# Attention and feed-forward on one core: the first pairs pinned in program order, values on four array tiles, second weights in three areas

## The chip, the core and the metric

The kernel runs on one core of a Trainium2 chip. The metric is the device time of one execution in microseconds. The core has five engines that the text names: TensorE (PE; its weight loads are PEld), VectorE (DVE), ScalarE (ACT), GpSimd (POOL) and SyncE (SP), whose queue issues all the DMAs here.

## The reference, cut to what matters

```python
scores = scale * np.matmul(q, k.transpose(0, 1, 3, 2))      # 8 batches, 8 heads, 576 positions, 64 wide
rel = pos[:, None] - pos[None, :]
mask_local = (rel >= 0) & (rel < 32)                        # heads 0 to 3
mask_strided = (rel >= 0) & (pos[None, :] % 32 == pos[:, None] % 32)   # heads 4 to 7
attn = softmax(np.where(masks, scores, -1e9))
x = (attn @ v).transpose(0, 2, 1, 3).reshape(4608, 512)
h = x @ w_in                                                # 512 x 2048
g = h * (1.0 / (1.0 + np.exp(-1.702 * h)))
return g @ w_out                                            # 2048 x 512
```

## The kernel before, in words

**Attention** is cut into 48 pairs of two units each (`_pairs`, line 55): for each of the eight batches three strided pairs and three local ones, in turn. A unit is a third of the positions of a batch (local) or a sixth of the residues (strided), of four heads. For a pair `scores` (169) multiplies queries and keys in windows into two PSUM banks; `softmax` (185) is a generator in five parts: mask and maximum on VectorE, subtraction on GpSimd (L212), exp on ScalarE (L214), sum and reciprocal on VectorE (L216 to L218), multiplication on GpSimd (L220). `turn` (223) transposes the probabilities on TensorE and copies them (L230). `values` (232) multiplies them with the values into one bank, and ScalarE copies the result into the five areas of x (L258, L267). The two heads of a group, j = 0 and 1, lie on partitions 0 to 63 and 64 to 127 of queries, keys, probabilities and values, and the result of head j goes to partitions 64j to 64j+63: a 64x64 tile of the array on its diagonal.

**The first product** (x with w_in) is done with seven products in place of eight, each in three terms of high and low halves (`product`, 330; 42 matmuls of 288 columns a block). There are eight blocks of w_in (pairs of 128 columns) and eight batches: 64 block products, numbered n, in passes of eight. `combine` (344) adds the seven up and writes the hidden rows to DRAM. `x_part` (282) splits the seven inputs of a batch, `x_sums` (277) makes two of the sums in them.

**Weights** come as 64-bit words, one block a megabyte: `w_convert` (300) makes them 32-bit floats, two operations on ScalarE (L303, L304) and one on VectorE (L307); `w_sums` (311) makes four sums on GpSimd (L316); `w_split` (320) splits all seven into high and low, two casts on ScalarE (L325) and two subtractions (L327), one of 768 columns on GpSimd and one of 1024 on VectorE. Raw blocks and split blocks share a pool of nine slots. The w_out blocks are read into the arena, over areas that attention no longer needs (`raw_at`, 105).

**The second product** (18 sets of 256 rows, four steps each) reads the hidden rows back (`load_g`, 467), applies the activation, sums and splits them (`prep`, 480) and multiplies with w_out (`products`, 508; `finish`, 522).

**The order.** The six pairs of batch 0 come first, in a loop of their own (line 394), with weight blocks 0 and 1 among them. The rest is a list of steps (line 551): a step holds one of the seven products of a block, and `side` (425) hangs other work on a step: the pairs of the next batch, the preparation of w_in blocks 2 to 7 in pass 0, that of the w_out blocks in the last pass. Only matmuls and transposes are kept in the order written (`keep_in_program_order` ties an instruction to the one written just ahead of it on its engine). All else is put into each engine's order by the framework's planner, which goes by its own estimate of times, takes work that is ready, and prefers what was written earlier.

Of the kernel before, what the change touches and what calls it, by code (L numbers as in the profile page):

```python
# [9 lines left out]
F32 = mybir.dt.float32  # L10
# [58 lines left out]
def attn_ffn(ctx, tc, qk, vs, weights, masks, ident, out):  # L69
# [6 lines left out]
    vector, scalar, gpsimd, sync = nc.vector, nc.scalar, nc.gpsimd, nc.sync  # L76

    def matmul(*args, **kw):
        tc.keep_in_program_order(nc.tensor.matmul(*args, **kw))  # L79

    def transposed(*args, **kw):
        tc.keep_in_program_order(nc.tensor.transpose(*args, **kw))
# [12 lines left out]
    prs = cut(AT_PR, 512, 2)  # L95
# [50 lines left out]
    qks, vts = {}, {}  # L146

    def load_qk(p):
        if p < len(pairs):
            nq, nk = _size(pairs[p][0])  # L150
            n = 4 * (nq + nk)
            t = qks_at[p % 2][:, :n]
            qks[p] = t.rearrange("p (i n) -> p i n", i=4)
            sync.dma_start(out=t, in_=qk[p][:, :n])

    def load_v(p):
        if p < len(pairs):
            n = 4 * (3 if pairs[p][0] == "l" else 2) * D
            t = vts_at[p % 2][:, :n]
# [25 lines left out]
    def softmax(p, banks):  # L185
        kind, _, c = pairs[p]
        nq, nk = (QL, WL) if kind == "l" else (QS, WS)
        pr = prs[p % 2].rearrange("p (i j n) -> p i j n", i=4, j=2)
        heads = prs[p % 2].rearrange("p (h n) -> p h n", h=8)[:nq, :, :nk]
# [33 lines left out]
    def turn(p, bank):  # L223
        nq = _size(pairs[p][0])[0]
        for i in range(4):
            transposed(
                bank[:, i * nq : (i + 1) * nq], prs[p % 2][:nq, i * P : (i + 1) * P],
# [4 lines left out]
    def values(p, bank):  # L232
# [5 lines left out]
        for i in range(4):  # L238
            for w, (q0, n, _, nk) in enumerate(windows(kind)):
                o = i * n0 + (q0 if kind == "l" else w * WS)  # L240
                if kind == "s":
                    n = min(n0, (w + 1) * WS) - w * WS
                for j in range(2):
                    rows = slice(j * D, j * D + nk)
                    matmul(
                        bank[j * D : (j + 1) * D, o : o + n],
                        lhsT=v[rows, i, w, :], rhs=pt[rows, i * nq + q0 : i * nq + q0 + n],
                        start=True, stop=True,
                    )
        x = {k: xr[k].rearrange("p (g n) -> p g n", g=2) for k in ("11", "12", "21", "22")}  # L250
        if kind == "l":
            src = bank[:, : 4 * QL].rearrange("p (g u n) -> p g u n", g=2, u=U)
            for h, cs in (("11", [c + u for u in range(U) if c + u < 3]),
                          ("21", [c + u for u in range(U) if c + u >= 3])):
                if cs:
                    u0, o = cs[0] - c, cs[0] % 3 * QL
                    n = len(cs)
                    scalar.copy(  # L258
                        out=x[h][:, :, o : o + n * QL].rearrange("p g (u n) -> p g u n", u=n),
                        in_=src[:, :, u0 : u0 + n],  # L260
                    )
            return
        n, r0, half = U * RES[c], R0[c], NPOS // 2
        src = bank[:, : 4 * n0].rearrange("p (g r t) -> p g t r", g=2, r=n)
        for k, h in enumerate(("12", "22")):
            o = x[h].rearrange("p g (t r) -> p g t r", r=STRIDE)[:, :, :, r0 : r0 + n]
            scalar.copy(out=o, in_=src[:, :, k * half : (k + 1) * half])  # L267
# [102 lines left out]


    load_qk(0)
# [11 lines left out]

    load_w(0)
    load_w(1)
    all_banks = [m_banks[i][x] for x in ("mx", "my", "mz") for i in range(2)]

    def start_banks(p):
        return all_banks[2 * (p % 2) : 2 * (p % 2) + 2]  # L390
# [277 lines left out]
```

## Time and profile before

| | us |
|---|---|
| median of three runs | 964.99 |
| lowest and highest run | 962.55, 965.57 |
| the profiled execution | 962.21 |
| its span on the core | 960.4 |
| TensorE busy in the span | 869.0 |
| VectorE, ScalarE, GpSimd busy | 619.5, 431.3, 501.9 |

The profile is of one execution. The span is what the engines' records cover; about 2 us of the execution's time lie around it. Busy time is the union of an engine's instructions; a matmul's end is modelled, so a busy TensorE is not one at its peak. The passes can be told apart by the writes of hidden rows: the windows below are cut where the writes of blocks 7 and 47 had been issued, at the first product (84.00), at the last pass and at the second stage.

### The profile page before, as it was taken

To read this page: it belongs to the slowest core of one execution; us is meant where nothing else is said; L and a number is where in the kernel's file an instruction comes from. 1 tells how busy PE (TensorE), PEld (TensorE's weight loads), DVE (VectorE), ACT (ScalarE), POOL (GpSimd) and SP (SyncE) were. 2 spreads that over 40 slices of the span, in tenths; PEclk is the share of its full clock that TensorE was granted. 3 is DMA by queue.
4 is the path that set the end of the run, shared out by engine and by line. 5 is a ranking of instruction groups with operands and counts; after the bars stand their busy time and mean duration, and the time that the engine had idled before them with its cause. 6 is when DMAs were issued, how large, how long until landed. Compare 5 with 4: busy or idle time off the path is not lost. (4 is left out here: it accounts for less than half of the span.)

```text
span 960.4 us, 23493 instructions
## 1 busy us (share of the span) xinstructions
PE 869.0 (90%) x9744; PEld 841.1 (88%) x9744; DVE 619.5 (64%) x1055; ACT 431.3 (45%) x733; POOL 501.9 (52%) x486
## 2 busy tenths in 40 slices
PE   3027999999999999999998985999999999999998
PEld 2026999999999999999998985999999999999998
DVE  5776548566474575754755786576767767677665
ACT  4644324233242232322424565555656556564552
POOL 5984213222132132222322699787777877877763
PEclk9999999999999999999999998899999999999999
DMA  9232444544444444354444575344343443434431
GB/s 374 94 112 65 158 148 159 165 162 147 153 159 146 157 162 153 131 178 146 160 137 141 205 252 170 100 145 141 117 136 123 146 142 113 140 121 145 142 110 44
DMA packets 78282, 141.68 MB, mean 148 GB/s; under 512 B 5856, under 2 KB 42848, under 8 KB 76128
## 3 DMA queue, kind: packets, MB, share of 16 engines
q1 hardware_dynamic: 78176, 140.19, 43.8%
q8 instruction: 76, 1.25, 0.5%
q14 instruction: 30, 0.25, 0.1%
HBM read 92.98 MB, written 47.19 MB: 146 GB/s over the span
## 5 line engine op out<-in xcount | busy, mean ns | idle before, releaser
L79 PE MATMUL my<-xa,w 128*128 128x288 f32 x1152 | 186.5, 303 | 10.3 <-ACT xa L272 4.4
L499 DVE TENSOR_TENSOR xa<-arena,xa 128x512 fp32r<-128x512 f32 (+1 forms) x144 | 140.8, 1005 | 81.7 <-ACT xa L498 81.3
L79 PEld LDWEIGHTS my<-xa,w 128*128 128x128 f32 x1152 | 162.6, 191 | 14.4 <-ACT xa L272 4.8
L484 ACT ACTIVATE arena<-arena 128x1024 f32<-128x1024 f32 x72 | 76.4, 1061 | 142.9 <-DMA arena<-hid 136.9
L79 PE MATMUL mx<-xa,w 128*128 128x288 f32 x768 | 129.4, 304 | 2.2 <-ACT arena L354 1.9
L79 PE MATMUL mz<-xa,w 128*128 128x288 f32 x768 | 126.9, 301 | 1.1 <-DVE arena L351 1.1
L212 POOL TENSOR_TENSOR arena<-arena,nmax 128x432 f32<-128x432 f32 (+1 forms) x48 | 51.4, 1070 | 140.4 <-DVE nmax L206 138.5
L351 DVE TENSOR_TENSOR arena<-my,arena 128x288 f32<-128x288 f32 x192 | 85.4, 452 | 49.1 <-PE my L79 48.7
L79 PEld LDWEIGHTS mx<-xa,w 128*128 128x128 f32 x768 | 110.0, 192 | 5.3 <-ACT arena L354 2.6
L79 PEld LDWEIGHTS mz<-xa,w 128*128 128x128 f32 x768 | 109.0, 190 | 2.8 <-DVE arena L351 1.7
L351 DVE TENSOR_TENSOR arena<-mz,arena 128x288 f32<-128x288 f32 x128 | 57.9, 453 | 80.1 <-PE mz L79 79.0
L220 POOL TENSOR_TENSOR arena<-arena,rinv 128x432 f32<-128x432 f32 (+1 forms) x48 | 50.7, 1055 | 110.9 <-DVE rinv L218 92.0
L491 POOL TENSOR_TENSOR arena<-arena 128x256 f32<-128x256 f32 x72 | 60.6, 842 | 84.1 <-DVE xa L499 55.7
L79 PEld LDWEIGHTS s<-arena 64*64 64x64 f32 (+2 forms) x3600 | 90.4, 133 | 15.4 <-issue 13.6
L79 PE MATMUL s<-arena 64*64 64x32 f32 (+4 forms) x3600 | 102.2, 227 | 0.2 <-DMA arena<-vs 0.2
L498 ACT CAST xa<-arena 128x512 fp32r<-128x512 f32 (+1 forms) x144 | 91.0, 685 | 11.2 <-POOL arena L494 10.3
L79 PE MATMUL my<-w,xa 128*128 128x256 f32 x576 | 84.4, 282 | 9.5 <-ACT xa L498 7.2
L499 DVE TENSOR_TENSOR ga<-arena,ga 128x512 fp32r<-128x512 f32 (+2 forms) x72 | 72.3, 1029 | 29.1 <-ACT ga L498 28.9
L79 PEld LDWEIGHTS my<-w,xa 128*128 128x128 f32 x576 | 75.2, 190 | 10.0 <-ACT xa L498 7.4
L79 PE MATMUL mx<-w,xa 128*128 128x256 f32 x576 | 83.8, 281 | 0.0
L79 PE MATMUL mz<-w,xa 128*128 128x256 f32 x576 | 83.7, 281 | 0.0
L492 POOL TENSOR_TENSOR arena<-arena 128x256 f32<-128x256 f32 x72 | 82.7, 1148 | 0.0
(71 smaller groups left out, 1445.8 us busy)
## 6 DMA issues: line engine op xcount, KB each, us to landing
hid<-arena SPq DMA_DIRECT2D x64, 576.0 KB, 3.4
arena<-hid SPq DMA_DIRECT2D x144, 256.0 KB, 3.3
arena<-qk SPq DMA_DIRECT2D x24, 472.0 KB, 4.2
arena<-qk SPq DMA_DIRECT2D x24, 448.0 KB, 3.9
arena<-vs SPq DMA_DIRECT2D x24, 384.0 KB, 3.2
out<-arena SPq DMA_DIRECT2D x36, 256.0 KB, 2.2
raw<-w_in SPq DMA_DIRECT2D x8, 1024.0 KB, 9.8
arena<-w_out SPq DMA_DIRECT2D x8, 1024.0 KB, 6.1
```

The costliest lines, as they stand in the source:

```text
L79: tc.keep_in_program_order(nc.tensor.matmul(*args, **kw))
L212: gpsimd.tensor_tensor(out=heads, in0=heads, in1=over(nmax), op=ALU.add)
L220: gpsimd.tensor_tensor(out=heads, in0=heads, in1=over(rinv), op=ALU.mult)
L351: vector.tensor_tensor(out=o, in0=x, in1=y, op=ALU.add)
L484: scalar.activation(g, g, AF.Gelu_apprx_sigmoid)
L491: gpsimd.tensor_tensor(out=s1, in0=a21, in1=a22, op=ALU.add)
L492: gpsimd.tensor_tensor(out=s2, in0=s1, in1=a11, op=ALU.subtract)
L498: scalar.copy(out=hi, in_=src)
L499: vector.tensor_tensor(out=lo, in0=src, in1=hi.bitcast(F32), op=ALU.subtract)
```

## The change

Four things are done.

1. Until the first batch's x is split, every instruction of every engine, SP's DMAs too, is tied to the one written ahead of it. The loop over the first six pairs is rewritten: one iteration holds the scores of pair i, the transposes of i-2, the values of i-3, the last two parts of the softmax of i-1 and the first three of i, and in iterations 2 to 7 one of the three steps of a weight block (0, then 1). The inputs of pairs 2 to 5 get space of their own, in two slots of the weight pool, and are loaded ahead. There is a third buffer for probabilities. The load of w_in block 2 is written behind the first batch's split.
2. In `values`, the second unit of a pair has its heads swapped on the partitions (the host lays it out so), so that head j is read from partitions 64(1-j) and written to 64j: the two other tiles. Each unit has a bank of its own, and ScalarE copies each unit by itself.
3. Both subtractions of `w_split` are on VectorE.
4. The w_out blocks: block 0 is read into a slot of the pool, the others into three areas in turn, one of them two blocks a step earlier in the list. Steps are shifted: pairs of pass 0 every 7 steps instead of 6, values in later passes one step earlier, `w_split` of blocks 2 to 7 two steps later.

```diff
+    class InOrder:
...
+            def ordered(*args, **kw):
+                ins = call(*args, **kw)
+                if self.strict[0]:
+                    tc.keep_in_program_order(ins)
+                return ins
...
+    strict = [True]
+    vector, scalar, gpsimd, sync = (
+        InOrder(e, strict) for e in (nc.vector, nc.scalar, nc.gpsimd, nc.sync)
+    )
+    tensor = InOrder(nc.tensor, [True])
+    matmul, transposed = tensor.matmul, tensor.transpose
...
-    prs = cut(AT_PR, 512, 2)
+    prs = cut(AT_PR, 512, 2) + cut(AT_H, 512, 1)
...
-    raw_at = spots(2048, 4096, 0, 2048)
-    gi_at = spots(1024, 6144, 2048, 4096, 5120)
-    s_at = spots(1024, 7168, 3072)
-    o_at = spots(512, 0, 512, 1024, 1536)
+    raw_at = spots(2048, 2048, 4096, 0)
+    gi_at = spots(1024, 6144, 0, 2048, 3072)
+    s_at = spots(1024, 7168, 1024)
+    o_at = spots(512, 4096, 4608, 5120, 5632)
...
+    def inputs(p):
+
+        if not 2 <= p < PAIRS:
+            return qks_at[p % 2], vts_at[p % 2]
+        if p // 2 not in early:
+            early[p // 2] = wp.tile([P, WLEN], F32, tag="w", name=f"early_{p // 2}", bufs=FP + 1)
+        t, n = early[p // 2], NQK + NV
+        return [t[:, p % 2 * n + a : p % 2 * n + b] for a, b in ((0, NQK), (NQK, n))]
...
+        for g in range(2):
             for w, (q0, n, _, nk) in enumerate(windows(kind)):
...
+                for u in range(U):
+                    i = U * g + u
+                    o = g * n0 + (q0 if kind == "l" else w * WS)
+                    for j in range(2):
+                        slot = j ^ u
+                        rows = slice(slot * D, slot * D + nk)
+                        matmul(
+                            banks[u][j * D : (j + 1) * D, o : o + n],
+                            lhsT=v[rows, i, w, :], rhs=pt[rows, i * nq + q0 : i * nq + q0 + n],
+                            start=True, stop=True,
+                        )
...
+        for u in range(U):
+            src = banks[u][:, : 2 * n0].rearrange("p (g n) -> p g n", g=2)
+            if kind == "l":
+                h, o = divmod(c + u, 3)
+                scalar.copy(out=x[("11", "21")[h]][:, :, o * QL : (o + 1) * QL], in_=src)
+                continue
+            n, r0, half = RES[c], R0[c + u], NPOS // 2
+            src = src.rearrange("p g (r t) -> p g t r", r=n)
+            for k, h in enumerate(("12", "22")):
+                o = x[h].rearrange("p g (t r) -> p g t r", r=STRIDE)[:, :, :, r0 : r0 + n]
+                scalar.copy(out=o, in_=src[:, :, k * half : (k + 1) * half])
...
-            low = vector if ks.start else gpsimd
-            low.tensor_tensor(out=lo, in0=src, in1=hi.bitcast(F32), op=ALU.subtract)
+            vector.tensor_tensor(out=lo, in0=src, in1=hi.bitcast(F32), op=ALU.subtract)
...
     load_v(0)
+    load_qk(2)
     load_v(1)
...
     load_w(0)
+    for i in range(3, n0):
+        load_qk(i)
+        load_v(i - 1)
+    load_v(n0 - 1)
     load_w(1)
...
     for i in range(n0 + 3):
         if i < n0:
-            scores(i, start_banks(i))
-            for _ in softmax(i, start_banks(i)):
-                pass
-            load_qk(i + 2)
+            ss = all_banks[2 * (i % 2) : 2 * (i % 2) + 2]
+            scores(i, ss)
+            firsts[i] = softmax(i, ss)
+            if i < 2:
+                load_qk(n0 + i)
+        if 2 <= i <= n0 + 1:
+            turn(i - 2, all_banks[4 + i % 2])
+        if i >= 3:
+            values(i - 3, s_banks)
+            if i < 5:
+                load_v(n0 + i - 3)
         if 1 <= i <= n0:
...
+            next(firsts[i - 1])
+            next(firsts[i - 1])
+        if i < n0:
+            for _ in range(3):
+                next(firsts[i])
+        if 2 <= i < 8:
+            weigh((i - 2) // 3, (i - 2) % 3)
...
-            s, t = (b * PASS - 9 + 8 * i, 11) if b else (6 * i, 9)
+            s, t, t2 = (b * PASS - 9 + 8 * i, 11, 14) if b else (7 * i, 10, 12)
...
-            side(s + t + 4, values, p, s_banks[1])
-            side(s + t + 4, load_v, p + 2)
+            side(s + t2, values, p, s_banks)
+            side(s + t2, load_v, p + 2)
...
-        side(STEP * (i - 2) + 4, lambda i=i: w_split(i, raws[i]))
-        side(STEP * (i - 2), load_w, i + 2)
+        side(STEP * (i - 2) + 6, lambda i=i: w_split(i, raws[i]))
+        if i > 2:
+            side(STEP * (i - 3) + 1, load_w, i)
...
     for k in range(7):
         x_part(k)
+    strict[0] = False
+    load_w(2)
...
-        at = (-9, 7, 7)[i] if i < 3 else STEP * (i - 3) + 14
-        side(last + at, lambda i=i: raws.update({i: w_words(1, i, raw_at[i % 3].bitcast(U32))}))
+        at = (-40, -9, 7, 7)[i] if i < 4 else STEP * (i - 3) + 14
+
+        def load_out(i=i):
+            raw = raw_at[i % 3].bitcast(U32) if i else raw_tile("raw_out")
+            raws[i] = w_words(1, i, raw)
+
+        side(last + at, load_out)
...
-    side(last + 1, ga_views)
+    side(last + 14, ga_views)
```

`weigh(i, step)` calls `w_convert`, `w_sums` or `w_split` of block i for step 0, 1 or 2.

## Rows read from the trace of the kernel before

**Rows 1.** The page, busy time of TensorE (share of the span, instructions).

```profile
PE 869.0 (90%) x9744; PEld 841.1 (88%) x9744; DVE 619.5 (64%) x1055; ACT 431.3 (45%) x733; POOL 501.9 (52%) x486
```

**Rows 2.** Windows: length, busy us (instructions) per engine, granted clock, DMA share, GB/s.

```profile
0.00:84.00 84.00, 25.96 (x505) 22.57 (x505) 55.38 (x56) 43.47 (x58) 63.56 (x58) 1.00 0.46 174
84.00:159.49 75.49, 71.24 (x983) 67.14 (x982) 47.68 (x103) 25.31 (x55) 22.25 (x19) 1.00 0.42 138
159.49:469.98 310.49, 305.70 (x4201) 291.34 (x4201) 189.06 (x426) 98.86 (x225) 78.79 (x70) 1.00 0.46 155
...
527.45:585.80 58.35, 51.48 (x341) 48.56 (x342) 44.79 (x62) 36.76 (x51) 48.31 (x38) 0.94 0.65 226
585.80:613.15 27.35, 17.88 (x127) 17.38 (x127) 16.23 (x16) 16.91 (x22) 24.88 (x24) 0.81 0.37 118
613.15:960.40 347.25, 342.71 (x2900) 342.51 (x2898) 236.16 (x328) 189.50 (x282) 251.19 (x266) 1.00 0.40 125
```

**Rows 3.** Timeline of TensorE, the start: start, us, what, [idle before <- releaser].

```profile
16.55 1.12 PE L79 MATMUL mx<-arena 64*64 64x54 f32 x32 [3.79 <-DMA arena<-qk]
...
46.52 1.12 PE L82 MATMUL mz<-ident_sb,arena 128*128 128x128 f32 x4 [24.40 <-POOL arena L220]
```

**Rows 4.** Groups by line, first 84 us: count, busy us, mean ns, idle before.

```profile
L316 POOL TENSOR_TENSOR raw<-raw 128x256 f32<-128x256 f32 x32 | 32.1, 1029 | 3.4 <-DVE raw L307 3.4
L307 DVE SCALAR_TENSOR_TENSOR raw<-raw 128x1024 uint32<-128x1024 uint32 x8 | 17.8, 2224 | 10.8 <-ACT raw L304 10.8
L325 ACT CAST w<-raw 128x768 fp32r<-128x768 f32 (+1 forms) x16 | 15.9, 1012 | 15.7 <-DVE raw L307 6.0 <-DVE w L327 5.5 <-POOL raw L316 4.2
L327 DVE TENSOR_TENSOR w<-raw,w 128x1024 fp32r<-128x1024 f32 x8 | 15.9, 1989 | 2.7 <-ACT w L325 2.3 <-POOL raw L316 0.3
L327 POOL TENSOR_TENSOR w<-raw,w 128x768 fp32r<-128x768 f32 x8 | 15.7, 1968 | 3.2 <-ACT w L325 3.2
...
L303 ACT ACTIVATE raw<-raw 128x1024 f32<-128x1024 f32 x8 | 9.3, 1160 | 8.6 <-DMA raw<-w_in 8.6
```

**Rows 5.** One line's instructions: ns min/median/max, first and last start.

```profile
L307 DVE SCALAR_TENSOR_TENSOR raw<-raw x8: 1226/1660/6735, 12.5 to 62.4; 128x1024 uint32<-128x1024 uint32 x8
...
L327 DVE TENSOR_TENSOR w<-arena,w x8: 1218/1516/2755, 538.2 to 597.2; 128x1024 fp32r<-128x1024 f32 x8
```

**Rows 6.** Timeline of SP's queue: the writes of blocks 7 and 47.

```profile
158.97 0.52 SPq L368 DMA_DIRECT2D hid<-arena  x1
...
469.46 0.52 SPq L368 DMA_DIRECT2D hid<-arena  x1
```

**Rows 7.** Groups of GpSimd by line, the last pass, 527.45 to 585.80 us.

```profile
L316 POOL TENSOR_TENSOR arena<-arena 128x256 f32<-128x256 f32 x28 | 31.5, 1146 | 9.7 <-DVE arena L307 9.5
L327 POOL TENSOR_TENSOR w<-arena,w 128x768 fp32r<-128x768 f32 x7 | 14.8, 2119 | 0.0
```

**Rows 8.** Timeline of TensorE, the second set's first wait.

```profile
599.04 0.80 PE L79 MATMUL my<-w,xa 128*128 128x256 f32 x2 [7.17 <-ACT xa L498]
```

**Rows 9.** Timeline of VectorE, the first pair.

```profile
5.36 0.67 DVE L200 SCALAR_TENSOR_TENSOR arena<-mx,masks_sb 128x216 f32<-128x216 f32 x2 [4.49 <-PE mx L79]
...
8.35 0.60 DVE L216 TENSOR_REDUCE ssum<-arena 128x8 f32<-128x432 f32 x1 [0.97 <-ACT arena L214]
...
9.66 0.20 DVE L218 RECIPROCAL rinv<-rinv 128x8 f32<-128x8 f32 x1
```

**Rows 10.** The page, GB/s that the DMA engines moved, 40 slices of 24 us.

```profile
GB/s 374 94 112 65 158 148 159 165 162 147 153 159 146 157 162 153 131 178 146 160 137 141 205 252 170 100 145 141 117 136 123 146 142 113 140 121 145 142 110 44
```

**Rows 11.** Timeline of TensorE, attention beside pass 1: values, scores, values.

```profile
158.18 1.14 PE L79 MATMUL s<-arena 54*64 54x54 f32 x32
...
160.24 0.80 PE L79 MATMUL s<-arena 64*64 64x54 f32 x32
...
167.10 1.59 PE L79 MATMUL s<-arena 64*64 64x32 f32 x48
```

**Rows 12.** The copies of strided values on ScalarE: ns min/median/max.

```profile
L267 ACT COPY arena<-s x48: 294/320/377, 29.4 to 506.5; 128x180 f32<-128x180 f32 x32, 128x216 f32<-128x216 f32 x16
```

More of the change, by code (lines that the diff above doesn't have):

```diff
@@ L74, in attn_ffn, with __init__, __getattr__ @@
     dram = ctx.enter_context(tc.tile_pool(name="dram", bufs=1, space=bass.MemoryType.DRAM))
[L76 to L82, printed above, removed]
+    class InOrder:
+        def __init__(self, engine, strict):
+            self.engine, self.strict = engine, strict
+        def __getattr__(self, name):
+            call = getattr(self.engine, name)
+            def ordered(*args, **kw):
[3 more added lines that the diff above has]
+                return ins
+            return ordered
+    strict = [True]
[4 more added lines that the diff above has]
+    matmul, transposed = tensor.matmul, tensor.transpose
     hid = dram.tile([FP, P, 2, B * S], F32, name="hid")
@@ L142, in attn_ffn, with pr_of @@
         gpsimd.memset(x, 0.0)
-    qks, vts = {}, {}
+    qks, vts, early = {}, {}, {}
+    def pr_of(p):
+        return prs[p % 3 if p < PAIRS else p % 2]
+    def inputs(p):
[5 more added lines that the diff above has]
+        return [t[:, p % 2 * n + a : p % 2 * n + b] for a, b in ((0, NQK), (NQK, n))]
     def load_qk(p):
@@ L151, in load_qk @@
             n = 4 * (nq + nk)
-            t = qks_at[p % 2][:, :n]
+            t = inputs(p)[0][:, :n]
             qks[p] = t.rearrange("p (i n) -> p i n", i=4)
@@ L158, in load_v @@
             n = 4 * (3 if pairs[p][0] == "l" else 2) * D
-            t = vts_at[p % 2][:, :n]
+            t = inputs(p)[1][:, :n]
             vts[p] = t.rearrange("p (i w d) -> p i w d", i=4, d=D)
@@ L230, in turn, with values @@
         scalar.copy(out=pts[p % 2][:, : 4 * nq], in_=bank[:, : 4 * nq])
-    def values(p, bank):
+    def values(p, banks):
         kind, b, c = pairs[p]
@@ L237, in values @@
         n0 = QL if kind == "l" else RES[c] * NPOS
-        for i in range(4):
+        for g in range(2):
             for w, (q0, n, _, nk) in enumerate(windows(kind)):
-                o = i * n0 + (q0 if kind == "l" else w * WS)
                 if kind == "s":
                     n = min(n0, (w + 1) * WS) - w * WS
[L243 to L249, printed above, removed]
@@ L250, in values @@
-        x = {k: xr[k].rearrange("p (g n) -> p g n", g=2) for k in ("11", "12", "21", "22")}
[L251 to L267, printed above, removed]
+                for u in range(U):
[9 more added lines that the diff above has]
+                        )
@@ L368, in combine, with load_w @@
             sync.dma_start(out=hid[i][:, :, b * S : (b + 1) * S], in_=h)
+    raws = {}
+    def load_w(i):
+        if i < FP:
+            raws[i] = w_words(0, i, raw_tile(f"raw_{i}"))
+    n0 = PAIRS
     load_qk(0)
@@ L376, in attn_ffn, with weigh @@
     load_v(0)
+    load_qk(2)
     load_v(1)
[L379 to L383 removed]
     load_w(0)
+    for i in range(3, n0):
+        load_qk(i)
+        load_v(i - 1)
+    load_v(n0 - 1)
     load_w(1)
     all_banks = [m_banks[i][x] for x in ("mx", "my", "mz") for i in range(2)]
[L389 to L393 removed]
+    def weigh(i, step):
+        if step == 0:
+            w_convert(raws[i])
+        elif step == 1:
+            w_sums(raws[i])
+        else:
+            w_split(i, raws[i])
+    firsts = {}
     for i in range(n0 + 3):
         if i < n0:
[L396 to L415 removed]
+            ss = all_banks[2 * (i % 2) : 2 * (i % 2) + 2]
[9 more added lines that the diff above has]
+                load_v(n0 + i - 3)
+        if 1 <= i <= n0:
+            next(firsts[i - 1])
[5 more added lines that the diff above has]
+            weigh((i - 2) // 3, (i - 2) % 3)
     sides, softs = {}, {}
```

30 lines of the change are left out of this document (5 added, 25 removed).

## The prediction, made before the changed kernel was run

> **What bounds the kernel now.** I read the page first: TensorE is busy 869.0 of 960.4 us [rows 1], so whatever shortens TensorE's stream or fills its holes is worth its full time. Then the windows by stage, to find the holes [rows 2]. There are three kinds of stretch.
>
> The start, up to the first product at 84.00: TensorE is busy 26.0 us of 84, VectorE 55.4, GpSimd 63.6. TensorE's own rows there show whom it waits for: an input load at 16.55, then 24.40 us for GpSimd's L220 at 46.52 [rows 3]. Grouped by line, GpSimd's time is not attention: 32 of L316 (32.1 us) and eight of L327 (15.7 us) are the preparation of all eight w_in blocks [rows 4], although the program places six of them in pass 0. The planner pulls them ahead, and the six pairs queue behind them. VectorE pays too: L307 takes 1226 ns at its shortest and 6735 at its longest [rows 5], mean 2224 [rows 4].
>
> The passes with attention beside them: TensorE is busy 305.7 of 310.5 us in five of them, at full clock [rows 2], from the write of block 7 to that of block 47 [rows 6]. That is 62.1 us a pass, bound by TensorE alone (VectorE 61%, ScalarE 32%).
>
> The change of stage: the last pass takes 58.35 us, and the next 27.35 us, mostly the second stage's first, hold only 127 matmuls at a mean granted clock of 0.81, so partly at the lower of its two levels [rows 2]. In the second stage 2900 matmuls of 256 columns take 347.25 us, 0.120 us each; by columns one of 288 is 0.135 us, a block of 42 is 5.7 us and the last pass would be 45.2 us alone. So 13 us are lost there, and 27.35 - 127 x 0.120 = 12 us behind it. In the last pass GpSimd is busy 48.3 of 58.35 us [rows 2]: 31.5 us of L316 and 14.8 us of seven L327 [rows 7]. Then TensorE waits 7.17 us for the operands of the second set [rows 8].
>
> All sums are against the profiled execution, 962.2 us (span 960.4); the median of the runs is 965.0, the lowest 962.55.
>
> **Part 1, the start.** Pinning holds six pairs and two weight blocks in the written order. The loop that sets its length runs mask, maximum, subtraction, exp, sum and reciprocal, since VectorE sums pair i-1 ahead of masking pair i. From the first mask at 5.36 to the first sum at 8.35 is 2.99 us; sum 0.60 and two small operations of about 0.2 make 4.0 us a pair [rows 9]. Six pairs: 5.4 + 6 x 4.0 = 29.4. Into this go two blocks of weights, in order: conversion 2 x 1.16 on ScalarE and 1.23 on VectorE, 3.5 us, all in the loop; four sums, which GpSimd does while VectorE masks, at 1.03 us each 4.1 us, of which I count half; the split, a cast of 1.01 and then two subtractions, together some 3.2 us [rows 4, 5]. That is 8.8 us a block, 17.6 for two. The drain behind the last reciprocal (multiplication, transposes, copy, values, copies, the first part of x) is about eight operations of 0.5 to 1 us, 6 us. First product at 29.4 + 17.6 + 6 = 53, against 84.00: 31 us.
>
> The inputs: four query-key and four value loads leave their double buffers for two slots of the weight pool and are issued ahead; 3.1 MB at the first slice's 374 GB/s [rows 10] is 8 us, by which w_in block 1 comes later. It is wanted by the sixth pair, after 30 us, so I take nothing; without that cover it would cost 8. SP's later loads in the pinned order wait for scores 0 and values 0; behind them stands only w_in block 2, wanted after 60 us. The third probability buffer adds one memset on an idle GpSimd: nothing.
>
> Given back in pass 0: six blocks of weights now fall beside it. VectorE is busy 47.7 of its 75.5 us [rows 2]. Six times 1.23 for L307 and 1.22 x 1.75 for the subtraction of 1792 columns (1.22 is the shortest of 1024 [rows 5]), all now on VectorE, is 20 us undisturbed; at the means of the start (2.2 and 2.0 x 1.75) it is 34 [rows 4]. That makes 68 to 82 us in a window of 75.5: pass 0 is between no longer and 7 longer, I take 3, since the planner will still pull some of these blocks into the holes of the start. Net gain 31 - 3 = 28. Ends: 12, where the start's work is as crowded as now (12 us more in its 53) and pass 0 loses 7; 38, where half of the weights' 17.6 hides in the loop and pass 0 loses 2.
>
> **Part 2, the values.** They now use four 64x64 tiles where they used two. Strided values, 32 matmuls, 16 on each tile, take 1.14 us; local ones, 48, 24 on each, 1.59 [rows 11]. The difference over eight is 56 ns a turn of a tile, over a fixed 0.24. The strided scores, 32 on four tiles, eight on each, take 0.80, where 0.24 + 8 x 0.056 is 0.69: four tiles do run side by side. So local values fall by 12 x 56 ns = 0.68 us, strided ones by 0.34 (by the scores' 0.80) to 0.45. Three of each a pass: 3.2 us, in six full passes 19; what pass 0 saves lies in its VectorE-bound stretch. Ends 10 (every second turn is lost) and 21 (0.45 for strided ones, rounded up).
>
> The Trainium skill has two rules on this: TensorEngine Tiling (Array Packing), Key Properties, lets different tiles load weights and multiply in parallel, and TensorE: Matmul & The Clock Gate, Part 3, says that a weight load overlaps a running matmul only when the row group differs. The new order visits row groups 0, 1, 1, 0; by the second rule this part could be 0 instead of 19, and the scores' row speaks for the first.
>
> ScalarE evacuates by unit: 18 copies a batch instead of 10. At 0.32 us [rows 12] eight more are 2.6 us a pass on an engine a third busy; hidden by the products between values and the next scores (below for when not). The shifted steps (pairs every 7 in pass 0, values one step earlier in later passes) and the mirrored order of the second unit, made on the host, put no work on any engine.
>
> **Part 3, the second weights.** L327's subtraction of 768 columns leaves GpSimd for VectorE in all 16 blocks. In the last pass GpSimd falls by 14.8 us to 34; VectorE rises from 44.8 by seven times 1.22 x 0.75, to 51 [rows 2, 5, 7], less L307 of the block that now goes to a pool slot and can be loaded and converted in an earlier pass (1.2 us). So VectorE near 50 bounds it in place of GpSimd: 58.35 becomes about 50, gain 8. Behind it, the operands of the second set are late because GpSimd and the areas are late; of the 12 us lost I take back half, 6. Gain 14; ends 4 (VectorE as crowded takes GpSimd's place) and 22 (13 and 9 of what is lost).
>
> **Sum:** 28 + 19 + 14 = 61, so 962.2 - 61 = 901; with half of the 2.8 us to the median, 902 us.
>
> **Rivals.** (a) The start stays crowded. A pin ties a marked instruction to what was written ahead of it, not the unmarked weight work behind it, which may still be planned into every hole. Three free slots of the pool let blocks 2 to 4 in. For it: that is what fills the 84 us now. Against it: the pairs no longer wait for loads (3.79 us at 16.55 [rows 3]), so there are fewer holes. If all of part 1 goes: 962.2 - 33 = 929. Chance 0.13.
>
> (b) Four tiles run as two because consecutive matmuls share a row group: 962.2 - 42 = 920. The scores' 0.80 us speaks against it, though their order alternates row groups where the new one does not. By the second rule above the Trainium skill would expect this one. Chance 0.12.
>
> (c) Slower: the values fill both score banks, and the next scores, two products (2 x 0.81 us) later, wait for ScalarE. Four copies of 0.32 us are 1.3 us; if each time some 2 us of ScalarE's other work stands ahead of them (six operations of that size), they end 3.2 us after the values: a wait of 1.6 us in each of 42 pairs, 67 us, gives 968. It decides from 61 / 42 = 1.45 us a pair. Against it: ScalarE is only a third busy in these passes, so such a queue is rare. Chance 0.06.
>
> The forecast has 0.69. The range goes from 880 (38, 21 and 22 would give 881) to 936, which takes in (a), (b) and the low ends of 12, 10 and 4. About 0.3%, 3 us, can be told from no change with this kernel; faster by more holds in the forecast, (a) and (b), 0.93 after 0.01 for no change; slower 0.06.
>
> **What would show it.** First product of the main stage near 53 instead of 84 us; L316 of fewer than eight blocks ahead of it; the wait for L220 gone. Pass 0 near 78 us with VectorE close to full. In the full passes local values near 0.9 us and strided near 0.7 to 0.8 instead of 1.59 and 1.14, and 59 us a pass. The last pass near 50 us, GpSimd near 34 in it. Wrong if the start again holds all 32 of L316, if the values' turns stay at two tiles, or if TensorE's waits before scores name ScalarE's copies.

## The result and the profile after

The changed kernel takes 926.29 us (median of four runs, 922.92 to 928.98) against 963.77 for the kernel before beside it: a ratio of 0.961, 95% interval 0.957 to 0.966. The forecast was 902 in a range of 880 to 936. The profile of one kernel below, no_pins_in_turn, is of an execution with TensorE at a lower granted clock (958.55 us), so its time below is the median of its other three (920.13 to 920.87), and its profile is read for order and waits up to the end of pass 0 alone.

The page of the kernel after, busy time, answers to [rows 1]:

```profile
PE 848.7 (92%) x9744; PEld 814.9 (88%) x9744; DVE 619.6 (67%) x1071; ACT 432.7 (47%) x797; POOL 478.3 (52%) x471
```

Windows of the kernel after, cut at the same events as [rows 2] (one row more, between block 47's write and the last pass; columns as there):

```profile
0.00:47.38 47.38, 20.01 (x504) 16.55 (x504) 20.17 (x43) 19.14 (x42) 19.29 (x27) 1.00 0.67 249
47.38:147.70 100.32, 75.26 (x986) 68.77 (x986) 76.20 (x128) 51.73 (x92) 59.79 (x48) 0.91 0.41 142
147.70:443.54 295.84, 289.40 (x4199) 274.34 (x4200) 188.88 (x424) 100.68 (x265) 78.32 (x70) 1.00 0.48 163
443.54:497.27 53.73, 50.86 (x693) 48.25 (x692) 30.22 (x69) 20.87 (x51) 12.88 (x13) 1.00 0.47 161
497.27:555.77 58.50, 49.29 (x341) 46.38 (x342) 49.70 (x69) 36.94 (x51) 37.54 (x30) 0.98 0.59 207
555.77:573.75 17.98, 17.43 (x127) 17.02 (x127) 13.35 (x14) 11.50 (x15) 16.97 (x18) 0.88 0.54 163
573.75:927.20 353.45, 346.47 (x2900) 343.61 (x2898) 241.08 (x330) 191.83 (x285) 253.50 (x269) 1.00 0.40 124
```

Before the change, the sixth pass with attention beside it, which [rows 2] leaves out:

```profile
469.98:527.45 57.47, 54.02 (x696) 51.61 (x695) 30.16 (x69) 20.46 (x42) 12.90 (x13) 1.00 0.44 151
```

Read by rows, after less before: the start 36.6 us shorter, pass 0 24.8 longer, five passes 14.6 shorter and the sixth 3.7 shorter, the last pass 0.2 longer, the next stretch of 127 matmuls 9.4 shorter, the second stage 6.2 longer. Together 33.2 us, the difference of the spans.

What pass 0 lost has one large piece. Timeline of TensorE after, then of GpSimd, around it:

```profile
67.41 1.03 PE L85 MATMUL my<-xa,w 128*128 128x288 f32 x6 [0.68 <-DVE arena L85]
81.56 1.11 PE L85 MATMUL s<-ident_sb,arena 128*128 128x128 f32 x4 [13.12 <-POOL arena L85]
```

```profile
63.92 1.89 POOL L85 TENSOR_TENSOR arena<-arena,nmax 128x432 f32<-128x432 f32 x1
65.77 13.87 POOL L85 TENSOR_TENSOR raw<-raw 128x256 f32<-128x256 f32 x9
...
80.60 0.90 POOL L85 TENSOR_TENSOR arena<-arena,rinv 128x432 f32<-128x432 f32 x1
```

(All lines are L85 now, since a helper records every call; forms and tiles tell them apart.) Pair 6 is subtracted at 63.92 and multiplied at 80.60; between them the planner put nine sums of later weight blocks. TensorE, whose order is fixed, stands at pair 6's transposes for 13.12 us.

The values, timeline of TensorE after, answer to [rows 11]:

```profile
113.97 0.90 PE L85 MATMUL s<-arena 64*64 64x32 f32 x48
...
121.87 0.67 PE L85 MATMUL s<-arena 54*64 54x54 f32 x32
```

Local values take 0.90 us in place of 1.59, strided ones 0.67 in place of 1.14. Twelve turns of a tile by the 56 ns and the fixed 0.24 of the prediction give 0.91, eight give 0.69: all four tiles work side by side. The rows decide between the two rules of the Trainium skill that the prediction set against each other. They agree with the Trainium skill's TensorEngine Tiling (Array Packing), Key Properties, by which different tiles work in parallel; by the Trainium skill's TensorE: Matmul & The Clock Gate, Part 3, every second turn, in row groups 0, 1, 1, 0, would not have overlapped.

In the last pass, ScalarE first, then TensorE:

```profile
508.87 2.16 ACT L85 ACTIVATE arena<-arena 128x1024 f32<-128x1024 f32 x2 [6.01 <-DMA arena<-w_out]
```

```profile
513.50 1.07 PE L85 MATMUL mx<-xa,w 128*128 128x288 f32 x6 [2.60 <-ACT arena L85]
```

ScalarE waits 6.01 us for a block of w_out with the conversion at the head of its queue, and the copy that TensorE needs is behind it. That is one of several waits. All of TensorE's longer ones in the last pass, by what ended them (us in total, times, longest us), name VectorE's sums for 5.5 us and ScalarE's copies for 3.5:

```profile
PE my L85 <- DVE arena L85: 4.1, 4, 1.9
PE mx L85 <- ACT arena L85: 3.5, 2, 2.6
PE mz L85 <- DVE arena L85: 1.4, 2, 0.7
```

### The profile page after: what moved, and what is told of

Read it like the earlier page. It is cut to its first block, busy times and chain, and to the rows that moved or that the text cites. A ratio compares the mean times of both kernels' runs of the same rounds, so it can differ in the third digit from the quotient of the medians.

```text
span 927.2 us, 23622 instructions
## 1 busy us (share of the span) xinstructions
PE 848.7 (92%) x9744; PEld 814.9 (88%) x9744; DVE 619.6 (67%) x1071; ACT 432.7 (47%) x797; POOL 478.3 (52%) x471
## 5 line engine op out<-in xcount | busy, mean ns | idle before, releaser
L85 POOL TENSOR_TENSOR arena<-arena 128x256 f32<-128x256 f32 (+1 forms) x332 | 336.2, 1037 | 181.8 <-DVE arena L85 83.9
L85 DVE TENSOR_TENSOR xa<-arena,xa 128x576 fp32r<-128x576 f32 (+3 forms) x200 | 198.4, 1016 | 72.8 <-ACT xa L85 72.4
L85 ACT ACTIVATE arena<-arena 128x1024 f32<-128x1024 f32 (+3 forms) x134 | 120.5, 905 | 222.2 <-DMA arena<-hid 139.1
L85 PE MATMUL my<-xa,w 128*128 128x288 f32 x1152 | 185.5, 302 | 13.1 <-DVE arena L85 8.1
L85 PEld LDWEIGHTS my<-xa,w 128*128 128x128 f32 x1152 | 161.0, 190 | 18.6 <-DVE arena L85 5.5
L85 PE MATMUL mx<-xa,w 128*128 128x288 f32 x768 | 131.0, 307 | 5.8 <-ACT arena L85 3.5
L85 ACT CAST xa<-arena 128x576 fp32r<-128x576 f32 (+3 forms) x200 | 127.4, 683 | 17.5 <-POOL arena L85 10.7
L85 PE MATMUL mz<-xa,w 128*128 128x288 f32 x768 | 127.6, 302 | 1.5 <-DVE arena L85 1.4
L85 ACT COPY arena<-mx 128x288 f32<-128x288 f32 (+1 forms) x146 | 57.5, 397 | 149.0 <-PE mx L85 95.4
L85 DVE TENSOR_TENSOR arena<-mz,arena 128x288 f32<-128x288 f32 (+1 forms) x182 | 80.1, 441 | 68.6 <-PE mz L85 68.1
L85 DVE TENSOR_TENSOR arena<-my,arena 128x288 f32<-128x288 f32 (+1 forms) x228 | 100.0, 445 | 38.6 <-PE my L85 37.3
L85 PEld LDWEIGHTS mx<-xa,w 128*128 128x128 f32 x768 | 111.5, 194 | 8.6 <-ACT arena L85 4.2
L85 POOL TENSOR_TENSOR arena<-arena,nmax 128x432 f32<-128x432 f32 (+1 forms) x48 | 50.3, 1049 | 124.7 <-DVE nmax L85 122.1
L85 PEld LDWEIGHTS mz<-xa,w 128*128 128x128 f32 x768 | 109.9, 191 | 3.6 <-DVE arena L85 2.4
L85 POOL TENSOR_TENSOR arena<-arena,rinv 128x432 f32<-128x432 f32 (+1 forms) x48 | 48.9, 1018 | 119.0 <-DVE rinv L85 119.0
L85 DVE TENSOR_TENSOR ga<-arena,ga 128x512 fp32r<-128x512 f32 (+2 forms) x72 | 73.0, 1038 | 33.3 <-ACT ga L85 33.0
L85 PE MATMUL my<-w,xa 128*128 128x256 f32 x576 | 85.7, 282 | 2.3 <-DVE xa L85 2.0
L85 ACT COPY arena<-s 128x90 f32<-128x90 f32 (+4 forms) x186 | 51.0, 336 | 70.9 <-PE s L85 64.3
L85 PE MATMUL mx<-w,xa 128*128 128x256 f32 x576 | 83.6, 280 | 0.0
L85 PE MATMUL mz<-w,xa 128*128 128x256 f32 x576 | 83.2, 280 | 0.0
L85 PEld LDWEIGHTS my<-w,xa 128*128 128x128 f32 x576 | 75.1, 188 | 4.1 <-DVE xa L85 3.9
L85 PEld LDWEIGHTS s<-arena 64*64 64x64 f32 (+2 forms) x3440 | 57.0, 130 | 22.5 <-issue 12.9
```

The source lines that it names most:

```text
L85: ins = call(*args, **kw)
```

## The experiments

Medians, the first product of the main stage and the end of block 7's write (from each trace, us). Two kernels with the same order on every engine to the end of pass 0 (pool_pinned_pass0, x_parts_pinned) differ by 3 us there, so less than that says nothing.

| kernel | median | first product | block 7 written |
|---|---|---|---|
| before | 963.8 | 84.0 | 159.5 |
| after | 926.3 | 47.4 | 147.7 |
| tiles_as_before | 946.6 | 48.8 | 150.7 |
| pool_pinned_pass0 | 917.4 | 47.3 | 139.9 |
| all_pinned_pass0 | 916.2 | 47.4 | 140.2 |
| x_parts_pinned | 918.3 | 47.3 | 142.9 |
| no_pins | 928.4 | 56.3 | 149.3 |
| inputs_in_turn | 935.0 | 49.7 | 158.2 |
| no_pins_in_turn | 920.4 | 67.3 | 145.5 |

In no_pins and no_pins_in_turn the first product is not yet the start of a steady stage: the second one, of which five matmuls wait for VectorE's split of x, comes at 79.3 and 77.1 us. After the change it comes at 54.6, with the hole of 13.12 us still ahead of it; before the change it came at 90.8:

```profile
90.75 1.57 PE L79 MATMUL my<-xa,w 128*128 128x288 f32 x5 [1.24 <-DVE xa L273]
```

### tiles_as_before: the values on two tiles again

```diff
-                        slot = j ^ u
+                        slot = j
```

(and the host's mirrored order of the second unit dropped)

> The changed kernel with the second unit of each pair back on the diagonal tiles: two array tiles in use instead of four, all else as changed. If the four tiles are what shortened the full passes (59.2 us instead of 62.1), they go back to 62 us: local values 1.6 us and strided 1.1 instead of 0.9 and 0.67, and the whole is 3 us x 6 = 17 to 20 us slower, about 944. If the shifted steps or the separate banks shortened them, the passes stay at 59 and the time at 926.

946.63 us, ratio 0.983 [0.980, 0.986]. Values in its timeline of TensorE:

```profile
147.29 1.14 PE L85 MATMUL s<-arena 54*64 54x54 f32 x32
...
157.18 1.59 PE L85 MATMUL s<-arena 64*64 64x32 f32 x48
```

Times of before, with the new banks, copies and steps kept. Five passes take 311.1 us (295.8 after, 310.5 before). So the tiles alone make the passes shorter, and the whole edit is worth 946.6 - 926.3 = 20 us.

### pool_pinned_pass0: GpSimd in program order to the end of pass 0

```diff
+        pool[0] = s < PASS
```

(the mark for program order is a list of its own for each engine)

> The changed kernel with GpSimd tied to the written order until the end of pass 0 (the other engines only until the first x is split). Theory: pass 0 takes 100 us because the planner puts nine sums of later weight blocks ahead of pair 6's multiplication on GpSimd, and TensorE, which is in order, waits 13.1 us at its transposes. Then this hole goes, pass 0 falls to about 85 us and the whole by 12 to 15, to about 912. Rival: pass 0 is bound by VectorE's 76 us and the late weights; then the wait moves to VectorE or to the weights, pass 0 stays above 95 and the time within 4 us of 926.

917.36 us, ratio 0.953 [0.950, 0.956]. Its windows and the row where the hole was:

```profile
0.00:47.27 47.27, 20.53 (x504) 16.83 (x504) 20.15 (x43) 19.12 (x42) 19.29 (x27) 1.00 0.66 250
47.27:139.90 92.63, 76.66 (x986) 69.83 (x986) 71.72 (x127) 51.25 (x90) 50.58 (x48) 0.94 0.45 154
```

```profile
70.93 0.66 PE L85 MATMUL s<-ident_sb,arena 128*128 128x128 f32 x4 [3.91 <-POOL arena L85]
```

The 13.12 us are 3.91, and pass 0 is 7.7 us shorter: GpSimd's order was the cause of that part. It did not reach 85. The second stage, from its first product to the end, takes 366.7 us for 371.4 after, though behind the first 127 matmuls every engine has the same instructions in the same order: TensorE's waits for VectorE that the profile shows in it are 1.1 us in three, 2.5 us in five after.

### all_pinned_pass0: every engine in program order to the end of pass 0

```diff
-    strict[0] = False
...
+        strict[0] = s < PASS
```

> The changed kernel with program order kept on all engines and on SyncE's queue until the end of pass 0, where pool_pinned_pass0 kept it on GpSimd alone (917.4 us, pass 0 92.6 us). Theory (only GpSimd's order was harmful; in program order ScalarE's and VectorE's short copies and adds stand behind whole blocks of weight work, as ScalarE's did in the last pass of act_pinned_last): pass 0 longer than 92.6 by 3 to 10 us, total 920 to 928. Rival (the planner's order is harmful on every engine in pass 0): pass 0 near 85 us, total near 910.

916.19 us, ratio 0.952 [0.947, 0.957], pass 0 92.8 us. Neither: on ScalarE and VectorE the written order is as good as the planner's. Its waits of TensorE in pass 0 (us in total, times, longest):

```profile
PE s L85 <- ACT arena L85: 8.6, 7, 2.1
PE my L85 <- DVE arena L85: 4.2, 3, 1.9
```

No long hole is left; many short ones are. This, pool_pinned_pass0 and x_parts_pinned are the fastest kernels of the study that do all the work.

### no_pins: no program order in the start

```diff
-    strict = [True]
+    strict = [False]
```

> The changed kernel with the marks for program order taken off VectorE, ScalarE, GpSimd and the queue of SyncE from the first instruction on; the inputs still come ahead and the loop over the first pairs is written as after the change. Theory (the order is what opened the start): weight blocks 2 to 6 go ahead of x_sums on GpSimd again (28 sums, 20 of them beyond those of blocks 0 and 1, about 1 us each), so the first product comes near 70 us against 47.4, pass 0 gets short in return (near 80 us against 100), and the total is near 926 + 23 - 20 = 929. Rival (the loads ahead are what opened it): first product below 53 us, pass 0 as it was, 926. Second rival: GpSimd's order in pass 0 is what costs, and with the weight work done ahead of it the hole goes: total below 920.

928.43 us, ratio 0.964 [0.962, 0.966]: as the theory had it in total (929). The first product is at 56.25, but it stands alone:

```profile
71.90 0.61 PE L85 MATMUL my<-xa,w 128*128 128x288 f32 x1 [8.17 <-ACT xa L85]
...
79.33 1.57 PE L85 MATMUL my<-xa,w 128*128 128x288 f32 x5 [6.83 <-DVE xa L85]
```

So the stage really begins near 79, after a start nearly as crowded as before, and pass 0 is quick in return. The marks bring the main stage's free run forward by some 25 us (54.6 for 79.3) and the end of pass 0 by 1.6, which is within the 3 us. The totals, 928.4 and 926.3, overlap in their runs.

### inputs_in_turn: no loads ahead

```diff
-        if not 2 <= p < PAIRS:
-            return qks_at[p % 2], vts_at[p % 2]
...
+        return qks_at[p % 2], vts_at[p % 2]
```

(`load_qk(i + 2)` and `load_v(i - 1)` in the loop)

> The changed kernel with the inputs of the first six pairs in the two old areas, loaded in turn as before the change (pair p + 2 when pair p is done), all else kept, program order too. Theory (the order opened the start, the loads ahead only cover a wait): each load is issued a whole turn of the loop ahead of its use, so the first product moves from 47.4 to between 47 and 51 us and the total from 926 to 926 to 930. Rival (the loads ahead are what opened the start): each turn waits for its load, some 4 us for each of four pairs, first product near 63 us, total near 942.

935.04 us, ratio 0.972 [0.969, 0.975]. The first product is where the theory put it, 49.7; the total is not. Pass 0 is 108.5 us long. TensorE's waits in it:

```profile
PE s L85 <- POOL arena L85: 13.6, 1, 13.6
PE s L85 <- ACT arena L85: 9.4, 4, 4.6
```

The same hole for GpSimd, and twice as much for ScalarE (4.8 us in four waits after, over the same stretch). Neither theory has this; how the loads change the order of ScalarE's work was not followed further.

### no_pins_in_turn: both put back

> The changed kernel with both put back: no marks for program order on VectorE, ScalarE, GpSimd and SyncE's queue, and the first six pairs' inputs in the two old areas, loaded in turn. Known from the two runs with one put back: without the marks the end of pass 0 (block 7's write) comes at 149.3 us, without the loads ahead at 158.2, with both kept at 147.7, and before the change at 159.5. Theory (the two add up, and the loop's new order gives nothing alone): block 7's write near 160 us, total near 937. Rival (each of them does the other's work in part, and with both gone the start is as crowded as before): 165 us or later, total 942 or more. Second rival (the marks cost with loads in turn): below 156 us, total below 932.

920.39 us, ratio 0.956 [0.951, 0.960]. The second rival: 920.13 to 920.87 lies below the lowest time of the changed kernel, 922.92. Its windows:

```profile
0.00:67.34 67.34, 20.72 (x504) 17.09 (x504) 54.85 (x60) 41.76 (x63) 53.43 (x51) 1.00 0.58 216
67.34:145.50 78.16, 70.94 (x985) 66.48 (x984) 53.25 (x109) 30.07 (x68) 25.24 (x23) 0.87 0.44 147
```

VectorE is as busy in the start as before (54.9 us, 55.4 in [rows 2]): nearly all the weight work is ahead again, GpSimd's 32 sums among it. But block 7 is written at 145.5 us instead of 159.5, no later than with both kept (147.7). So neither the marks nor the loads ahead bring the gain of the start and pass 0 together. Beside the marks the loads ahead gain 8.7 us of the total (935.0 to 926.3); without the marks they cost 8.0 (920.4 to 928.4). Where the rest of the 5.9 us between this kernel and the changed one lies, behind pass 0, cannot be read from this trace.

What is left for the gain are three things that this kernel shares with the changed one. The loop's order is new: a pair's softmax no longer has to end before the next begins (with the third buffer). The subtractions of 768 columns are VectorE's, which took 15.7 us of GpSimd's start before [rows 4]. The values run on four tiles, and TensorE is busy 20.7 us in the start instead of 26.0. TensorE's waits for GpSimd ahead of the transposes, before and in this kernel:

```profile
PE mz L82 <- POOL arena L220: 49.7, 5, 24.4
```

```profile
PE mz L85 <- POOL arena L85: 21.5, 4, 9.5
```

They fall by 28 us, which both the loop's order and a GpSimd with less to do would give; against that stand 12.7 us of waits for ScalarE ahead of the values, where there were none. None of the three was put back in the start, so which of them brings the gain is not shown.

### w_out_split_back: the 768-column subtraction of the second weights on GpSimd again

```diff
+            low = gp if gp and not ks.start else vector
```

> The changed kernel with one thing put back: the 768-column subtraction of each block of the second weights is GpSimd's again (8 of about 2.1 us), in the last pass alone. By the prediction (its third part: moving them to VectorE and the three areas end GpSimd's lateness, VectorE is the bound) the last pass should change by several us, either up by some 8 (GpSimd late again) or down by some 5 (VectorE relieved). Theory now: neither engine sets the last pass; ScalarE's copies and casts stand behind conversions that wait for the loads of the second weights, so last pass and total stay within 2 us of 58.5 and 926.

931.39 us, ratio 0.967 [0.965, 0.969]. Its windows of the last pass and behind it, and TensorE's longest wait there:

```profile
497.78:555.53 57.75, 49.09 (x338) 47.23 (x337) 43.94 (x61) 35.61 (x47) 46.60 (x35) 0.94 0.58 201
555.53:573.50 17.97, 9.44 (x58) 8.36 (x57) 11.04 (x12) 10.95 (x15) 15.83 (x16) 0.72 0.58 180
```

```profile
PE mx L85 <- ACT xa L85: 5.4, 1, 5.4
```

The theory held for the last pass (57.75 us; 58.50 after), though GpSimd is busy 46.6 in it instead of 37.5, but not for the total. Behind it 58 matmuls run in 18 us where 127 did, with a wait like that of [rows 8] back. Cut where the 127 have started, the second stage is:

```profile
555.53:583.41 27.88, 19.35 (x128) 18.27 (x127) 15.81 (x17) 15.97 (x21) 23.16 (x24) 0.76 0.44 135
583.41:930.70 347.29, 342.70 (x2900) 342.50 (x2898) 235.23 (x327) 190.49 (x282) 248.32 (x265) 1.00 0.41 125
```

The first 127 matmuls are back at the length of before (27.35 us in [rows 2], 17.98 after): for the second weights the move to VectorE pays there, 9.9 us, and not in the last pass. The rest takes 347.3 us, as before the change, where it took 353.4 after, and the total is 5.1 us longer. The move for w_in's blocks was not put back.

### last_no_weights: the last pass without work on the second weights

```diff
-        side(last + at + 5, lambda i=i: w_convert(raws[i]))
-        side(last + at + 5, lambda i=i: w_sums(raws[i]))
-        side(last + STEP * i + 13, lambda i=i: w_split(i, raws[i]))
+        side(last + STEP * i + 13, lambda i=i: w_fill(i))
```

> The changed kernel without the work on the second weights: their conversion, sums and splitting are left out (the loads stay), and GpSimd fills the eight weight tiles with zeros, so the second stage multiplies zeros. The last pass, from its first product at 497.27 to the second stage's first at 555.77, is 58.5 us with TensorE's groups of six products 0.79 us apart, 56 of them: 44.3 us. Theory (what the pass loses are single waits for copies and sums that stand behind the weights' long instructions on ScalarE and VectorE): without them the pass is 45 to 48 us, and the second stage starts at full pace, total 905 to 912. Rival (the chain of copies and sums of a block itself sets it, or the waits for GA's first sets): 54 us or more, total above 918.

907.34 us, ratio 0.942 [0.939, 0.946]. The last pass:

```profile
494.90:542.31 47.41, 45.55 (x339) 44.60 (x337) 26.61 (x53) 15.34 (x28) 27.81 (x17) 1.00 0.76 268
542.31:904.48 362.17, 357.59 (x3026) 357.39 (x3024) 243.05 (x337) 198.72 (x294) 261.28 (x277) 1.00 0.41 126
```

47.4 us instead of 58.5: 11 us are the weights' doing, and no engine was full in those 58.5 (VectorE 49.7, TensorE 49.3). The theory holds on the place; the next run asks what about them it is. The second stage (second row) is 9 us shorter besides, 362.2 us for 371.4 after. It multiplies zeros here, and whether the missing work or the zeros do that was not separated.

### weights_in_halves: the same work in shorter instructions

```diff
+        for p in range(parts):
+            q = slice(4 // parts * p, 4 // parts * (p + 1))
```

(conversion, casts and subtractions of the second weights, on top of pool_pinned_pass0)

> The kernel of pool_pinned_pass0 (917.4 us; block 55's write to the second stage's first product 52.95 us) with ScalarE's and VectorE's instructions on the second weights cut in two (two for each of the conversion, casts and subtractions of two of the seven parts at a time). Theory (short instructions of a block's sums wait for the long one that runs): the last pass shortens by 2 to 4 us, total 913 to 916. Rival (the fixed part of each instruction eats it): the last pass within 1 us or longer, total 917 to 921.

921.62 us, ratio 0.957 [0.953, 0.961]. From block 55's write to the second stage it is 57.2 us in place of 52.95. ScalarE's timeline in the last pass:

```profile
503.77 2.35 ACT L85 ACTIVATE arena<-arena 128x512 f32<-128x512 f32 x4 [4.43 <-DMA arena<-w_out]
...
522.96 2.39 ACT L85 ACTIVATE arena<-arena 128x512 f32<-128x512 f32 x4 [1.60 <-DMA arena<-w_out]
```

The halves run in fours behind the same kind of wait, and the total is 4 us worse: the theory fell, and the time is where the rival had it (917 to 921). Cutting the instructions does not help; what these rows point to is the head of ScalarE's queue, which waits for a load. Whether that or the fixed part of more instructions made the pass longer was not separated, and to move the loads themselves was not tried.

### act_pinned_last and x_parts_pinned: ScalarE in program order

```diff
+        act[0] = s >= last - 10
...
+        conv = 8 if i == 1 else at + 9
```

> The changed kernel with ScalarE tied to the written order in the last pass, and each conversion of w_out written 9 steps behind its load (5 before). Theory: the last pass gained nothing because ScalarE stands still on conversions whose load has not landed (6.0 us once, 3.2, 1.9), with copies of product banks queued behind, for which TensorE waits. Then the last pass falls from 58.5 to about 52 us, the whole to about 920. Rival: VectorE, 49.7 of 58.5 us busy, bounds the pass; then it stays at 57 to 59 and the time at 926.

934.49 us, ratio 0.971 [0.967, 0.974]. Block 55's write comes 55.6 us after block 47's instead of 59.9, but then, in its timelines of ScalarE and of TensorE:

```profile
546.25 1.04 ACT L85 CAST ga<-arena 128x1024 fp32r<-128x1024 f32 x1 [4.96 <-POOL arena L85]
...
549.01 0.40 ACT L85 COPY arena<-mx 128x288 f32<-128x288 f32 x1
```

```profile
549.46 1.81 PE L85 MATMUL mx<-xa,w 128*128 128x288 f32 x6 [8.45 <-ACT arena L85]
```

A cast waits for GpSimd, and a copy of 0.40 us, for which TensorE had long finished, stands behind it. The theory fell: what the first part of the pass gains is lost behind it, and the total is 8 us worse. The same with the marks from ten steps ahead of the last pass to its ninth step only, on top of pool_pinned_pass0:

```diff
+        pool[0], act[0] = s < PASS, last - 10 <= s < last + 9
```

> The kernel of pool_pinned_pass0 with ScalarE in program order besides from 10 steps ahead of the last pass to its ninth step, and the conversion of the second weights' blocks called later (block 1 at step 8, the others two steps after their load). Theory (the first part of the last pass loses time because ScalarE's conversion waits for a load of the second weights while casts of x stand behind it): block 55's write comes 55.5 to 56.5 us after block 47's (59.8 with GpSimd's order alone), the rest as in pool_pinned_pass0, total near 917.4 - 4 = 913.5. Rival (the time is lost again behind it, as with ScalarE pinned to the end): last pass longer by 4 or more, total 917 to 921.

918.27 us, ratio 0.953 [0.951, 0.956]: block 55's write 57.8 us behind block 47's (59.8), the total not told apart from 917.4. Half of the piece is gained and does not show.

### stage2_pinned: the second stage in program order

```diff
+    dve[0] = act[0] = pool[0] = True
     assert not sides, sorted(sides)
```

> The changed kernel with VectorE, ScalarE and GpSimd tied to the written order in the second stage. Theory: the second stage is 6 us longer than before because its operands come just in time (TensorE waits 0.2 to 0.8 us for VectorE some 13 times), which is the planner's order of preparing and adding up; in the written order the preparation stands two steps ahead, the waits go and the whole is about 920. Rival: VectorE and GpSimd slow each other, whatever the order; then the waits stay and the time is 926 or more.

965.67 us, ratio 1.002 [1.000, 1.004]. TensorE's waits in the second stage:

```profile
PE my L85 <- DVE xa L85: 15.1, 37, 0.8
PE my L85 <- DVE ga L85: 7.1, 17, 0.4
```

The theory fell: the stage is 37 us longer (408.6 for 371.4 after), and in the written order most steps are late by a little. As written, the activation of a step stands behind the last cast of the step ahead, which waits for GpSimd's sums (ScalarE's casts for xa wait 117.1 us for them, in 46 waits of at most 2.7); the planner's order is the better one here.

## Why the prediction came out as it did

The time lay in the range, 24 us above the forecast, and closer to the 929 of rival (a) than to the 902. It lay there by the width of the range and not by its parts: pass 0 came 24.8 us longer, where the upper end of that step was 7, the start gained 5.6 more than forecast, and the second stage, which the sum leaves out, lost 6.2. By its parts:

**Part 1, net 28 us: 11.8 came.** The start gained 36.6 for the 31 expected. The step that failed is "pass 0 is between no longer and 7 longer, I take 3": it was 24.8. VectorE's load was sized well (68 to 82 us expected, 76.2 measured), but the step took a pass to be as long as its fullest engine. GpSimd's 24 sums were not counted in it at all (its busy time went from 22.3 to 59.8 us), and the largest piece is where a block of such sums stands in the queue: one wait of 13.12 us, which is 3.91 with GpSimd's order fixed, in a pass 7.7 us shorter. The rest of what TensorE stands in pass 0 is shorter waits, 6.6 us for VectorE and 5.7 for ScalarE, where before the change there were 4.3 in all; what set these was not tested. TensorE's granted clock in pass 0 was 0.91, where [rows 2] has 1.00, and its busy time 4.0 us more. The reason given for the gain does not hold either: "Pinning holds six pairs and two weight blocks in the written order" is true, but without pins and loads ahead pass 0 ends no later and the kernel is 5.9 us faster (920.4). It is where the pins end that costs: with GpSimd's kept to the end of pass 0, the kernel with pins takes 917.4.

**Part 2, 19 us: right.** 18.4 us in six passes by the windows (14.6 and 3.7), 20 by tiles_as_before; 59.2 us a pass for the 59 expected. Rival (b) falls with the values' rows. Rival (c) needed 1.45 us a pair to decide; TensorE's waits before scores that name ScalarE's copies are 2.5 us in all five passes:

```profile
L85 PE MATMUL s<-arena 64*64 64x54 f32 x480 | 11.8, 223 | 2.5 <-ACT arena L85 2.5
```

**Part 3, 14 us: 9.2 came.** The failed step is "VectorE near 50 bounds it in place of GpSimd: 58.35 becomes about 50". VectorE did come to 49.7 and GpSimd to 37.5, and the pass stayed at 58.50: neither had bounded it. Its floor is TensorE's 44.3 us, 56 groups of 0.79, and without the second weights' work it is 47.4, as last_no_weights shows. So 11.1 of the 14.2 us that the pass takes above its floor are that work's doing, while no engine is full. That it comes by copies and sums standing behind weight work in the queues of ScalarE and VectorE is read from the waits and is not shown by a run: shorter instructions did not help, and ScalarE's order gained 2.0 us of the first piece and nothing in the total. Behind the pass 9.4 us came for the 6 expected, by the cause that was named (GpSimd's lateness), as w_out_split_back shows.

**Not in the sum:** 6.2 us in the second stage behind its first 127 matmuls. TensorE waits there 2.1 us for VectorE's subtractions, in four waits, where it waited for nothing before, and is busy 3.8 us longer. pool_pinned_pass0 has the same order there and 4.7 us less, and all_pinned_pass0, with the same order too, takes the 347.3 us of before:

```profile
567.53:914.80 347.27, 342.70 (x2900) 342.50 (x2898) 240.78 (x330) 192.04 (x285) 258.54 (x269) 1.00 0.41 126
```

So it is a matter of timing and not of the edit's instructions; why it falls so in one trace and not in the other stays open.

Rival (a) named the right mechanism, unmarked weight work planned into every hole, at the wrong place: it filled pass 0, not the start, where only the 8 sums of blocks 0 and 1 were left.

## What to carry to other kernels

In a kernel with in-order queues a stage is not as long as its fullest engine: look at what stands at the head of each queue, and what it waits for, with short work behind it that another engine needs. A mark that holds part of the work in order hands the rest to the planner, so ask where the unmarked work will go; moving preparation out of a start saves only what its new place can take without stopping the bound engine. And undo the parts of a change in pairs, not only one by one: here the loads ahead seemed to pay 8.7 us and the marks next to nothing, and without both the kernel is 5.9 us faster.

## What the runs showed of the hardware that was not expected

A sum of 256 columns on GpSimd takes 0.78 us in the start of the changed kernel, where VectorE is busy 20 of 47 us, and 13.87 / 9 = 1.54 us in the hole of pass 0:

```profile
L85 POOL TENSOR_TENSOR raw<-raw 128x256 f32<-128x256 f32 x8 | 6.1, 783 | 0.2
```

The eight again, then the nine of the hole, each with ns min/median/max and first and last start:

```profile
L85 POOL TENSOR_TENSOR raw<-raw x8: 606/841/847, 23.5 to 44.3; 128x256 f32<-128x256 f32 x8
```

```profile
L85 POOL TENSOR_TENSOR raw<-raw x9: 612/1597/2131, 65.8 to 78.4; 128x256 f32<-128x256 f32 x9
```

Beside VectorE's weight work a sum is thus twice as dear on GpSimd here; the prediction stretched VectorE's work for this, not GpSimd's. A busy VectorE alone does not do it: during three of the four sums from 23.50 to 26.64 us VectorE was busy nearly throughout, with reductions, small operations and masks, and none of the four took over 0.85. In the hole its time goes mostly to weight subtractions, shifts and sums. Which of its operations make the difference was not tested.

TensorE's granted clock is 0.70 in the window of the hole, where it stands for 13.12 us, and 1.00 ahead of it; the mean lies between its two levels, so it was at the lower one for part of that window:

```profile
47.38:65.00 17.62, 11.45 (x112) 9.60 (x113) 16.30 (x19) 13.11 (x17) 14.67 (x10) 1.00 0.25 89
65.00:82.50 17.50, 3.70 (x23) 3.26 (x23) 15.80 (x20) 10.39 (x12) 17.34 (x14) 0.70 0.41 147
```
